# Gate and up projections as seven products of halves, with their weights held in DRAM

## The chip, the core and the metric

The kernel runs on one core of a Trainium2 chip. A core has five engines, each with an instruction queue of its own: TensorE (PE in the profile; PEld is its loading of stationary weights), VectorE (DVE), ScalarE (ACT), GpSimd (POOL) and SyncE (SP), which here only issues DMAs. The core's SBUF holds working data in 128 partitions, PSUM takes TensorE's results in eight banks of 512 float32 columns, and DRAM holds inputs, output and spilled tensors. Sixteen DMA engines move data between DRAM and SBUF. The metric is the device time of one execution in microseconds (us).

## The reference

A block over 8192 tokens of 448 channels: an AFNO spectral mixer and a GEGLU feed-forward network, both with adaptive layer norm.

```python
h = layernorm(x) * (1 + ca) + sa
x = x + ga * A(h)        # rfft over tokens, per-frequency 2-layer MLP, shrinkage, irfft
h = layernorm(x) * (1 + cb) + sb
x = x + gb * ((gelu(h @ w_gate) * (h @ w_up)) @ w_down)    # 448 -> 1792 -> 448
```

The sizes are N = 8192, D = 448, F = 1792. sa to gb are rows of silu(c) @ w_mod. Everything is float32 at the interface; the kernel splits float32 factors into a high and a low 16-bit part and takes three products (high by high, high by low, low by high).

## The kernel before

The program has three stages on one core: the forward transform over chunks of x, a spectral stage of 32 steps, and the FFN stage, which also ends the inverse transform.

**Spectral stage.** `step(i)` writes out, in a fixed order, the work of one step: `fetch_t` (loads `tr`), `stage_s2` (second transform: groups of three products of 128 columns, L368 to L370), the two MLP layers, `stage_i1`, and hooks ("load", "pe", "act", "dve", "pool") into which `at(step, hook, fn, ...)` puts side work. In steps 3 to 14 the side work loads gate and up weights, squares them and sums the squares with products against ones (`norms`, L711), for scales. From step 17 on, `load_w` loads one piece of 256 columns of w_gate or w_up per step, and `weights_hi` (ACT, L790) and `weights_lo` (DVE, L795) cast it into the resident tiles `wh` and `wl`, [128, 4, 3584] in fp16 each.

**FFN stage.** The work goes by blocks of 256 tokens (`CB` = 2 rows of 128; 32 blocks, index i). Within a block, t counts seven pairs of 128 hidden channels, tile t and tile t + 7 (q = 0, 1). `gate_up(i, k)` with k = 2t + q multiplies 128 hidden channels of gate and of up (pr = 0, 1) with 256 tokens. The 448 input channels are three full groups of 128 rows and one of 64; the high and low parts of the last 64 are packed so that ten products of 128 rows and 256 columns do for gate or for up, and what is left of the low weights of the last 64 rows is done for two values of t together, as a burst of eight products of 64 rows, in the upper or lower half of the array (all at L1087). Gate goes through a gelu on ACT (L1123), times up on DVE (L1128).

The down projection takes 2 x 2 halves (hidden tiles t and t + 7, output column halves, two token rows) and computes seven products instead of eight. Its left factors are the four quarters and four sums of them, made on POOL (L1134 to L1137); `quantize` casts them into high (ACT, L1145) and low (DVE, L1146) parts. `down(i - 1)` runs after k = 2 of block i: 7 x 7 x 3 products of 224 columns (L1153 to L1155), with copies and sums (L1176 to L1194) and `finish`, on POOL, which scales, adds the residual and hands the rows to the output DMA (L1197).

**Preparing a block.** Tables `hooks`, `second`, `ahead` and `first` place, by k, the steps that prepare the block two ahead: `load_v`, `load_g` (DMA), `split_v`, `split_g` (ACT, POOL), `inverse` (L987 to L989, TensorE), `residual`, `stats2`, `rsqrt_part`, `norm2` (L1036, L1037), `pack_hi`, `pack_lo`, and `transposes_dma` (L1057), in which SP issues four DMA transposes per block into `nts`. For block 0 the transposes are done by TensorE (L1069). Six of the seven down weight tiles are loaded and cast (`load_d8`, `down_hi` L920, `down_lo` L924) during the first block.

The order is written out by hand: each engine runs its instructions in the order of the program. All DMAs go through SP's queue, also in program order. PSUM has four tags, pa to pd, of two banks each, which `bank` hands out in turn; gate and up use pa and pb, down uses pd and pc.

## Time and profile before

| | us |
|---|---|
| median of 3 runs | 1941.13 (1939.67 to 1942.28) |
| the profiled execution: time | 1940.48 |
| its span in the profile | 1938.7 |
| TensorE busy in the span | 1903.1 |
| DVE / ACT / POOL busy | 1109.8 / 788.3 / 1159.4 |
| first and last start of a gate or up product | 385.0 and 1919.4 |

In the profile, a row of a group gives line, engine, operation, the tiles (out<-in), the shape, the count after "x", then busy time in us, the mean duration of one in ns, and the idle time of the engine before them with what ended it. Busy time counts overlapping instructions once, so count times mean can be more. A row of the timeline gives the start, the duration in us, engine, line and operation; neighbours of one line are merged, with their count. A row of a stretch of time gives its ends, its length, each engine's busy time with its instructions, the granted TensorE clock, the DMA engines' busy share and GB/s. A row of one line's instructions gives minimum, median and maximum duration in ns and the first and last start.

### The profile page before, as it was taken

To read this page: it belongs to the slowest core of one execution; us is meant where nothing else is said; L and a number is where in the kernel's file an instruction comes from. 1 tells how busy PE (TensorE), PEld (TensorE's weight loads), DVE (VectorE), ACT (ScalarE), POOL (GpSimd) and SP (SyncE) were. 2 spreads that over 40 slices of the span, in tenths; PEclk is the share of its full clock that TensorE was granted. 3 is DMA by queue.
4 is the path that set the end of the run, shared out by engine and by line. 5 is a ranking of instruction groups with operands and counts; after the bars stand their busy time and mean duration, and the time that the engine had idled before them with its cause. 6 is when DMAs were issued, how large, how long until landed. Compare 5 with 4: busy or idle time off the path is not lost.

```text
span 1938.7 us, 43005 instructions
## 1 busy us (share of the span) xinstructions
PE 1903.1 (98%) x17620; PEld 1694.9 (87%) x17620; DVE 1109.8 (57%) x2352; ACT 788.3 (41%) x1338; POOL 1159.4 (60%) x1466
## 2 busy tenths in 40 slices
PE   7899999899999999999999999999999999999999
PEld 3599999778888888888888888888888888888898
DVE  8677788786555555555555555555555555555533
ACT  5677888553333333333333333333333333333322
POOL 3157655256666666666666666666666666666644
PEclk9899999999999999999999999999999999999999
...
GB/s 346 314 286 257 203 188 197 171 140 49 45 43 45 43 41 45 45 41 46 41 46 43 42 44 44 43 43 44 43 44 43 43 43 43 43 43 43 21 11 20
DMA packets 157981, 163.79 MB, mean 84 GB/s; under 512 B 77908, under 2 KB 136152, under 8 KB 157784
## 3 DMA queue, kind: packets, MB, share of 16 engines
...
## 4 chain that ended last, share of the span: by engine, by line
PE 86%; DVE 4%; issue 3%; ACT 3%; DMA 2%; POOL 2%; SPq 1%; ACTq 0%; POOLq 0%; DVEq 0%
PE pgu L1087 53%; PE pdn L1155 8%; PE pdn L1154 8%; PE pdn L1153 8%; PE ps L202 2%; DVE y L463 2%; PE pi L989 1%; PE pi L988 1%; PE pi L987 1%; POOL yl L107 1%; DMA raw<-in_B_w_up 1%; DVE st L163 0%; ACT th L105 0%; PE ps L368 0%; PE ps L370 0%
## 5 line engine op out<-in xcount | busy, mean ns | idle before, releaser
L1087 PE MATMUL pgu<-nt,wh 128*128 128x256 f16 x6272 | 834.3, 273 | 2.7 <-DVE x L1128 2.6
L1087 PEld LDWEIGHTS <-wh 128*128 128x128 f16 x6272 | 602.7, 98 | 101.5 <-issue 33.9
L1123 ACT ACTIVATE gel<-pgu,dg 128x256 f32<-128x256 f32 x448 | 200.3, 473 | 792.3 <-PE pgu L1087 756.2
L1087 PE MATMUL pgu<-nt,wl 128*128 128x256 f16 (+1 forms) x3584 | 501.3, 272 | 0.4 <-DVE x L1128 0.4
L1155 PE MATMUL pdn<-wd,ac 128*128 128x224 f16 x1568 | 406.1, 259 | 0.2 <-DVE ac L1146 0.2
L1153 PE MATMUL pdn<-wd,ac 128*128 128x224 f16 x1568 | 406.1, 259 | 0.0
L1154 PE MATMUL pdn<-wd,ac 128*128 128x224 f16 x1568 | 406.1, 259 | 0.0
L1134 POOL TENSOR_TENSOR x<-x 128x128 f32<-128x128 f32 x223 | 239.9, 1076 | 260.3 <-DVE x L1128 228.1
L1146 DVE SCALAR_TENSOR_TENSOR ac<-x,sa_act,ac 128x896 f16<-128x896 f32 (+1 forms) x225 | 308.9, 1373 | 83.3 <-ACT ac L1145 83.3
L1087 PEld LDWEIGHTS <-wl 128*128 128x128 f16 (+1 forms) x3584 | 297.9, 97 | 57.5 <-issue 24.3
L1128 DVE TENSOR_TENSOR x<-pgu,gel 128x256 f32<-128x256 f32 x448 | 179.6, 418 | 276.2 <-ACT gel L1123 275.6
L1145 ACT ACTIVATE ac<-x,sa_act 128x896 f16<-128x896 f32 (+1 forms) x225 | 232.9, 1035 | 49.0 <-POOL x L1137 47.0
L1190 POOL TENSOR_TENSOR o<-u,p 128x224 f32<-128x224 f32 x32 | 21.0, 657 | 291.8 <-DVE u L1189 291.8
L1135 POOL TENSOR_TENSOR x<-x 128x128 f32<-128x128 f32 x223 | 157.5, 706 | 17.5
L1155 PEld LDWEIGHTS <-ac 128*128 128x128 f16 x1568 | 153.4, 98 | 0.5 <-DVE ac L1146 0.5
L1154 PEld LDWEIGHTS <-ac 128*128 128x128 f16 x1568 | 153.4, 98 | 0.4
L1153 PEld LDWEIGHTS <-ac 128*128 128x128 f16 x1568 | 153.4, 98 | 0.4
L107 POOL TENSOR_TENSOR yl<-y,yh 128x448 fp32r<-128x448 f32 x63 | 78.9, 1252 | 75.6 <-ACT yh L105 64.4
L463 DVE SCALAR_TENSOR_TENSOR y<-pm,t 64x224 f32<-64x224 f32 x256 | 99.5, 389 | 41.3 <-ACT t L455 37.4
L1136 POOL TENSOR_TENSOR x<-x 128x128 f32<-128x128 f32 x223 | 113.7, 510 | 0.0
L1137 POOL TENSOR_TENSOR x<-x 128x128 f32<-128x128 f32 x223 | 110.7, 497 | 0.0
L107 POOL TENSOR_TENSOR tl<-tr,th 128x896 f16<-128x896 f32 x30 | 57.3, 1909 | 68.3 <-DMA td<-xt 36.8
...
## 6 DMA issues: line engine op xcount, KB each, us to landing
...
```

The lines of the kernel that those rows point to most:

```text
L107: (el or V).tensor_tensor(lo, src, h, ALU.subtract)
L463: V.scalar_tensor_tensor(y[ri * 64 : ri * 64 + 64, gi], pv[si, ri], LAM, tv[si, ri], op0=ALU.add, op1=ALU.min)
L1087: T.matmul(pgu[i, t, q][:, pr * H : (pr + 1) * H], w[rows, tw, f0 : f0 + 128], nts[i][rows, tn, :], start=start, stop=stop, skip_group_che ...
L1123: S.activation(gl, ps[:, :H], AF.Gelu_apprx_tanh, scale=dg)
L1128: V.tensor_tensor(dst, ps[:, H : 2 * H].rearrange("p (b c) -> p b c", b=2), gl.rearrange("p (b c) -> p b c", b=2), ALU.mult)
L1134: e.tensor_tensor(s1, a21, a22, ALU.add)
L1135: e.tensor_tensor(s2, s1, a11, ALU.subtract)
L1145: S.activation(ac[:, 0, k], x[:, k], AF.Copy, scale=sc)
L1146: V.scalar_tensor_tensor(ac[:, 1, k], x[:, k], sc, ac[:, 0, k], op0=ALU.mult, op1=ALU.subtract)
L1153: T.matmul(ps, ac[:, 0, ka], wds[t][:, 0, kb], start=t == 0, stop=False)
L1154: T.matmul(ps, ac[:, 0, ka], wds[t][:, 1, kb], start=False, stop=False)
L1155: T.matmul(ps, ac[:, 1, ka], wds[t][:, 0, kb], start=False, stop=t == NP - 1)
```

## The change

Gate and up are no longer multiplied by 128-row products. For 384 of the 448 channels, the product of (two halves of the channels) x (hidden tiles t and t + 7) x (two token rows) is formed as seven products of halves instead of eight; the last 64 channels are multiplied directly. The channels are cut into pieces of 64 rows: gate's weights lie in partitions 0 to 63 and up's in 64 to 127, each with its copy of the tokens, and every step of 64 rows issues a product for gate in the upper half of the array and one for up in the lower half, of 128 columns each, into two banks.

- **Weights.** In the spectral stage `load_forms` loads the pieces of one t, `form_sums` makes the sums of quarters (POOL), `forms_hi` and `forms_lo` cast 23 pieces of 128 columns, and `store_forms` writes them to DRAM (`wsd`). In the FFN stage three slots hold the forms of three t. `torder` runs through t upward and downward in turn; `plan_slots` says which slot is refilled for which later unit, and `after` issues the load in two parts (12 and 11 pieces) when stage b or stage d of the unit that frees it has been issued.
- **Tokens.** `token_sums` makes sums of token pieces (DVE), and `transposes` issues twelve DMA transposes per block instead of four, for block 0 too.
- **Order of a unit.** A unit u is one t of one block. Its products come in four stages: a, b, c, d. `period(u)` interleaves stage a of u, stage d of u - 2, stage c of u - 1 and stage b of u. Between them ACT copies partial results (`copy_b`), seeds one region of PSUM with another (`seed`), DVE joins regions (`joins`), and gelu and product go over three quarters and one quarter (`gel3`, `mult3`, `gel1`, `mult1`). Three pairs of banks (`sets`) go round by u mod 3, the fourth (`pdn`) is for down.
- **Down.** All seven tiles are cast in the spectral stage. `down` uses pdn and the set `pf`, which the following unit's stage a takes; `phase(i)` runs the inverse transform, the residual, the loads of the block after, and down, after the third unit of a block.
- The scales of tokens and of gate and up weights are made for a smaller range (13 in place of 15 as the exponent), and a DMA scratch area in SBUF is cut to 2048 bytes.

```diff
+        def load_forms(t):
+            r = fp.tile([128, 14, 128], F32, tag="wr", name="wr", bufs=2)
+            for pr, rows in enumerate(rows2):
+                v = (wg, wu)[pr].rearrange("(k p) (q t f) -> p q k t f", p=64, q=2, t=NP)
+                for q in range(2):
+                    dma(r[rows, 6 * q : 6 * q + 6], v[:, q, 0:6, t])
+                dma(r[rows, 12:14], v[:, :, 6, t])
+            return r
+
+        def form_sums(t):
+            r = raws[("w", t)]
+            f = raws[("f", t)] = fp.tile([128, 9, 128], F32, tag="wf", name="wf")
+            a11, a12, a21, a22 = (r[:, 3 * j : 3 * j + 3] for j in range(4))
+            G.tensor_tensor(f[:, 3:6], a11, a21, ALU.subtract)
+            G.tensor_tensor(a21, a21, a22, ALU.add)
+            G.tensor_tensor(f[:, 0:3], a21, a11, ALU.subtract)
+            G.tensor_tensor(f[:, 6:9], a12, f[:, 0:3], ALU.subtract)
+
+        def form_cuts(t, part):
+            r = raws[("w", t)]
+            if part == 0:
+                return (slice(0, 9), r[:, 0:9]), (slice(18, 23), r[:, 9:14])
+            return ((slice(9, 18), raws[("f", t)]),)
+
+        def forms_hi(t, part):
+            for k, src in form_cuts(t, part):
+                S.activation(wslot[wat[t]][:, 0, k], src, AF.Copy, scale=sww)
+
+        def forms_lo(t, part):
+            for k, src in form_cuts(t, part):
+                w = wslot[wat[t]]
+                V.scalar_tensor_tensor(w[:, 1, k], src, sww, w[:, 0, k], op0=ALU.mult, op1=ALU.subtract)
+
+        def store_forms(t):
+            a = 0
+            for w, n in zip(wsd, WPARTS):
+                dma(w[t], wslot[wat[t]][:, :, a : a + n])
+                a += n
 
         wdp = wd.rearrange("(q t p) c -> t p q c", q=2, p=128)
...
         wpool = ctx.enter_context(tc.tile_pool(name="wpool", bufs=1))
-        wh = wpool.tile([128, 4, 2 * F], F16, name="wh")
-        wl = wpool.tile([128, 4, 2 * F], F16, name="wl")
+        wslot = [wpool.tile([128, 2, NWB, 128], F16, name=f"ws{s}") for s in range(2)]
...
         at(19, "dve", down_scales2)
-        for j in range(14):
-            at(17 + j, "load", pre, fp, ("w", j % 2, j // 2), load_w, j % 2, j // 2)
-            at(18 + j, "act", weights_hi, j % 2, j // 2)
-            at(18 + j, "dve", weights_lo, j % 2, j // 2)
-        at(30, "load", load_d4, fp, 0)
+        for n, t in enumerate(worder):
+            u = 18 + 2 * n
+            at(max(17, u - 2), "load", pre, None, ("w", t), lambda pool, t: load_forms(t), t)
+            at(u - 1, "pool", form_sums, t)
+            for part in range(2):
+                at(u + part, "act", forms_hi, t, part)
+                at(u + part, "dve", forms_lo, t, part)
+            if u + 2 < nu:
+                at(u + 2, "load", store_forms, t)
+        for t, u in enumerate([21, 23, 25, 27, 29, 30, 31]):
+            at(u - 1, "load" if u < 30 else "pool", load_d4, t)
...
+        torder = [t for i in range(nch) for t in (range(NP) if i % 2 == 0 else range(NP - 1, -1, -1))]
+        slot_of, refill = {}, {}
...
+        def plan_slots():
+
+            held = [[0 if wat[0] == s else 1, -1] for s in range(2)] + [[2, -1]]
+            for u, t in enumerate(torder):
+                s = next((n for n, (h, _) in enumerate(held) if h == t), None)
+                if s is None:
+                    s = min(range(3), key=lambda n: held[n][1])
+                    refill[held[s][1]] = u
+                    held[s][0] = t
+                slot_of[u] = wslot[s]
+                held[s][1] = u
+
+        plan_slots()
+
+        def load_part(u, part):
+
+            a, n = (0, WPARTS[0]), WPARTS
+            lo = a[part]
+            dma(slot_of[u][:, :, lo : lo + n[part]], wsd[part][torder[u]])
+
+        def after(u, part):
+
+            if u in refill:
+                load_part(refill[u], part)
 
...
-        def transposes_dma(i, gs=range(2)):
+        def token_sums(i, part):
+
+            n = nxt[i]["n"]
+            if part == 0:
+                nxt[i]["t"] = cp.tile([128, 13 * 64], F32, tag="tf", name="tf")
+            t = nxt[i]["t"]
+            b11, b21, x0 = n[:, 0, 0:192], n[:, 0, 192:384], n[:, 0, 384:448]
+            b12, b22, x1 = n[:, 1, 0:192], n[:, 1, 192:384], n[:, 1, 384:448]
+            t1, t2, t3, t4 = (t[:, 192 * j : 192 * j + 192] for j in range(4))
+            if part == 0:
+                V.tensor_tensor(t1, b12, b11, ALU.subtract)
+                V.tensor_tensor(t3, b22, b12, ALU.subtract)
+            else:
+                V.tensor_tensor(t2, b22, t1, ALU.subtract)
+                V.tensor_tensor(t4, b21, t2, ALU.subtract)
...
+        def transposes(i, gs):
+            if i not in nts:
+                nts[i] = cp.tile([128, 2, NXT, 128], F16, tag="nt", name="nt", bufs=2)
             for g in gs:
-                for b in range(CB):
-                    nc.sync.dma_start(
-                        nts[i][:, 4 * g : 4 * g + 4, b * 128 : (b + 1) * 128],
-                        nxt[i]["pk"][:, b, PKO[4 * g] : PKO[4 * g] + 512],
-                        transpose=True,
-                    )
-
...
+        def xblock(i, pr, n):
+            w, odd = divmod(n, 2)
+            if odd == pr:
+                return nts[i][rows2[pr], 0, w, :]
+            return nts[i][rows2[pr], 1, w if odd else (w - 1) % NXT, :]
+
+        def mm(u, ps2, reg, wb, x, xo, n, start=False):
+
+            i, slot = u // NP, slot_of[u]
+            for j in range(n):
+                for m, (hl, xb) in enumerate(((0, x[0]), (0, x[1]), (1, x[0]))):
+                    for pr, rows in enumerate(rows2):
+                        T.matmul(
+                            ps2[:, pr, reg * 128 : reg * 128 + 128],
+                            slot[rows, hl, wb + j, :],
+                            xblock(i, pr, xb + xo + j),
+                            start=start and j == 0 and m == 0,
+                            stop=j == n - 1 and m == 2,
+                            skip_group_check=True,
+                        )
+
+        RV, RY, RX = 0, 1, 2
+
+        def stage_a(u):
+            p = sets[u % 3]
+            mm(u, p, RY, 0, XB0, 0, 3, start=True)
+            mm(u, p, RV, 6, XT, 0, 3)
+            mm(u, p, RX, 3, XB0, 3, 3)
+
+        def stage_b(u):
+            mm(u, sets[u % 3], RY, 9, XT, 3, 3)
+
+        def stage_c(u):
+            p = sets[u % 3]
+            mm(u, p, RV, 12, XT, 6, 3)
+            mm(u, p, RV, 22, XB1, 6, 1)
+            mm(u, p, RY, 15, XB1, 3, 3)
+            mm(u, p, RY, 21, XB1, 6, 1)
+            mm(u, p, RX, 21, XB0, 6, 1)
+
+        def stage_d(u):
+            p = sets[u % 3]
+            mm(u, p, RV, 18, XT, 9, 3)
+            mm(u, p, RV, 22, XT, 12, 1)
+
+        sbs, cts = {}, {}
...
+        def copy_b(u):
+            sbs[u] = cp.tile([128, 2, 256], F32, tag="sb", name="sb", bufs=2)
+            S.copy(sbs[u], sets[u % 3][:, :, 0:256])
+
+        def seed(u):
+            p = sets[u % 3]
+            S.copy(p[:, :, 0:128], p[:, :, 128:256])
+
+        def joins(u):
+            p, b = sets[u % 3], sbs.pop(u)
+            c = cts[u] = cp.tile([128, 2, 3, 128], F32, tag="c", name="c")
+            V.tensor_tensor(
+                c[:, :, 1:3, :],
+                p[:, :, 0:256].rearrange("p g (r c) -> p g r c", r=2),
+                b[:, :, 0:128].rearrange("p g (o c) -> p g o c", o=1).to_broadcast([128, 2, 2, 128]),
+                ALU.add,
             )
-
...
+        def gel3(u):
+            gls[u] = cp.tile([128, 3, 128], F32, tag="gl3", name="gl3")
+            S.activation(gls[u], cts[u][:, 0], AF.Gelu_apprx_tanh, scale=dg)
+
+        def mult3(u):
+            xs[u] = cp.tile([128, 8, 128], F32, tag="x8", name="x8", bufs=4)
+            V.tensor_tensor(xs[u][:, 1::3, :], cts.pop(u)[:, 1], gls.pop(u), ALU.mult)
+
+        def gel1(u):
+            gls[u] = cp.tile([128, 128], F32, tag="gl1", name="gl1", bufs=2)
+            S.activation(gls[u], sets[u % 3][:, 0, 0:128], AF.Gelu_apprx_tanh, scale=dg)
+
+        def mult1(u):
+            V.tensor_tensor(xs[u][:, 0], sets[u % 3][:, 1, 0:128], gls.pop(u), ALU.mult)
+
+        def sums(u, e=G):
+            a12, a11, s1, s2, a22, s3, s4, a21 = (xs[u][:, j] for j in range(8))
+            e.tensor_tensor(s1, a21, a22, ALU.add)
...
-            b1, b2 = bank("pd", "pdn"), bank("pc", "pdn")
-
-            product(i, b1, 0, 0, range(NP - 1))
-            product(i, b2, 1, 1, range(NP - 1))
-            S.copy(p1, product(i, b1, 0, 0, [NP - 1]))
-            V.tensor_tensor(o11, product(i, b2, 1, 1, [NP - 1]), p1, ALU.add)
+            d0, d1, f0, f1 = (p[:, b, :] for p in (pdn, pf) for b in range(2))
+            heads = [(0, d0), (1, d1)] + ([(2, f0), (4, f1)] if last else [])
...
+            S.copy(p4, product(i, f0, 2, rest if last else range(NP)))
+            if not last:
+                mid(1)
+            V.tensor_tensor(u2, product(i, f1, 4, rest if last else range(NP)), p1, ALU.add)
+            V.tensor_tensor(u4, product(i, d0, 3), u2, ALU.add)
+            if not last:
+                mid(2)
+            p7 = product(i, d1, 5)
...
+            p3 = product(i, f0, 6)
             for b, h in ((1, 0), (1, 1), (0, 1)) if last else ((1, None), (0, None)):
                 if b == 0:
                     V.tensor_tensor(o12, p3, u4, ALU.add)
...
+        def period(u):
+            on(u, stage_a)
+            on(u - 1, seed)
+            on(u - 2, joins)
+            on(u - 2, gel3)
+            on(u - 4, quant_lo)
+            on(u - 2, mult3)
+            on(u, copy_b)
+            on(u - 2, stage_d)
+            on(u - 2, lambda v: after(v, 1))
+            on(u - 2, gel1)
+            on(u - 2, mult1)
+            on(u - 2, lambda v: sums(v, V if v == NT_ - 1 else G))
+            on(u - 3, quant_hi)
+            on(u - 1, stage_c)
+            on(u, stage_b)
+            on(u, lambda v: after(v, 0))
+
...
+        def phase(i):
+
+            u = i * NP + LA
+            pf = sets[(u + 1) % 3]
+            j = i + 2
+            on(u - 3, quant_lo)
+            if j < nch:
+                inverse(j, pf)
+                residual(j)
+                loads(j + 1)
...
+            if i > 0:
+                down(i - 1, pf, mid)
+
+        extra = {
+            0: [(2, split_v)],
+            1: [(2, split_g), (1, transposes, range(0, 4))],
+            2: [(1, transposes, range(4, 12))],
+            3: [(2, token_sums, 0), (2, pack_hi, [0]), (2, pack_lo, [0])],
+            4: [(2, token_sums, 1), (2, pack_hi, [1]), (2, pack_lo, [1])],
+            5: [(2, pack_hi, [2]), (2, pack_lo, [2])],
+            6: [(2, pack_hi, [3]), (2, pack_lo, [3])],
```

401 lines of the change are left out of this document (179 added, 222 removed).

## The prediction

> **What bounds the kernel now.** I read the page first (busy shares, then the chain), then long stretches, then single products in the timeline.
>
> ```profile
> span 1938.7 us, 43005 instructions
> PE 1903.1 (98%) x17620; PEld 1694.9 (87%) x17620; DVE 1109.8 (57%) x2352; ACT 788.3 (41%) x1338; POOL 1159.4 (60%) x1466
> PE pgu L1087 53%; PE pdn L1155 8%; PE pdn L1154 8%; PE pdn L1153 8%; PE ps L202 2%; DVE y L463 2%; PE pi L989 1%; PE pi L988 1%; PE pi L987 1%; POOL yl L107 1%; DMA raw<-in_B_w_up 1%; DVE st L163 0%; ACT th L105 0%; PE ps L368 0%; PE ps L370 0%
> ```
> ```profile
> 480.00:1890.00 1410.00, 1409.84 (x13488) 1263.11 (x13486) 725.21 (x1433) 455.62 (x756) 900.41 (x1162) 1.00 0.15 42
> ```
> The second fence is one stretch of the FFN: busy time of PE, weight loads, DVE, ACT, POOL, then the granted clock (1.00), the DMA share (0.15) and GB/s. TensorE is never free; the others are half idle or more. Gate and up are 53% of the chain, the down product 24%. A busy PE need not be at its peak, so its pace comes from starts in the timeline: ten full products, 256 columns each, then a stretch with a shared burst of half-height products (8 of the 11), the down product from its first start to the next gate product, and the inverse transform; below them, from SP's timeline, two starts of the transposes, three blocks apart.
>
> ```profile
> 1000.56 0.93 PE L1087 MATMUL pgu<-nt,wh 128*128 128x256 f16 x7
> 1001.32 0.49 PE L1087 MATMUL pgu<-nt,wl 128*128 128x256 f16 x3
> 1001.65 0.27 PE L1087 MATMUL pgu<-nt,wh 128*128 128x256 f16 x1
> ...
> 1004.60 1.03 PE L1087 MATMUL pgu<-nt,wl 128*128 128x256 f16 x11
> 1005.56 0.50 PE L1087 MATMUL pgu<-nt,wh 128*128 128x256 f16 x3
> ...
> 1012.12 0.26 PE L1153 MATMUL pdn<-wd,ac 128*128 128x224 f16 x1
> ...
> 1026.21 0.49 PE L1087 MATMUL pgu<-nt,wh 128*128 128x256 f16 x3
> ...
> 1035.52 0.45 PE L987 MATMUL pi<-vh,gh 128*128 128x448 f32 x1
> ...
> 1036.84 0.94 PE L1087 MATMUL pgu<-nt,wh 128*128 128x256 f16 x7
> ```
> ```profile
> 867.02 6.40 SPq L1057 DMA_TRANSPOSE nt<-pk  x4
> ...
> 1011.37 5.13 SPq L1057 DMA_TRANSPOSE nt<-pk  x4
> ```
> Ten products take 1001.65 − 1000.56 = 1.09 us, 109 ns each. A block has 7 x 40 of them: 30.5 us. A burst costs 1005.56 − 1004.60 less three full products, 0.63 us; 3.5 per block: 2.2 us. Down takes 14.1 us, the inverse transform 1.3. Sum 48.1; the transposes say (1011.37 − 867.02)/3 = 48.1. Nothing but products is in a block.
>
> **The change: TensorE.** A unit (a block's pair of 128-channel tiles t and t+7) now has 25 steps of 64 rows in stages a (9), b (3), c (9), d (4), each in three high/low products for gate and for up: 75 pairs of 64-row, 128-column products, 16,800 pairs in all. What a pair costs decides the case. The trace has pairs at 256 columns (the half bursts), 128-column products at full height (L368 to L370), and dense loads (the norms):
>
> ```profile
> L1087 PE MATMUL pgu<-nt,wl 64*128 64x256 f16 x896 | 68.6, 272 | 0.4 <-DVE x L1128 0.4
> L711 PEld LDWEIGHTS <-sq 128*128 128x128 bf16 x84 | 4.1, 97 | 1.1 <-issue 0.2
> 345.83 0.22 PE L369 MATMUL ps<-s,th 128*112 128x128 f16 x1
> ...
> 346.90 0.22 PE L370 MATMUL ps<-s,tl 128*112 128x128 f16 x1
> ```
> The 896 half products are 112 bursts of 8 and fill 68.6 us, 0.61 us a burst; one after another 8 would need 7 x 0.109 + 0.27 = 1.03, as four pairs 3 x 0.109 + 0.27 = 0.60. So halves do run two at a time. From 345.83 to 346.90 are 19 intervals: 56 ns for 128 columns, a new weight load each. I take 56 ns per pair: 525 pairs per block = 29.6 us against 30.5 + 2.2. The unseen part is that four instructions must start per 56 ns, where these rows sustain two. L711 gives the nearest dense case: 28 groups of three loads fill 4.1 us, (4.1/28 − 0.097)/2 = 25 ns from load to load with a product between, two in 50 ns; that is why I take 56. The ends are 50 ns and 112 ns, the latter (+941 us) if starts keep today's two per 56.
>
> Each burst's two changes between full and half height cost (0.63 − 4 x 0.109)/2 = 0.1 us; instead of 3.5 round trips a block there is one around the inverse and down: +0.1 beside the row above, the return lying under the next wait. Down's last product now goes to a bank of the set that the next stage a fills, so TensorE waits for L1194 to empty it: the rest of that product (0.26 us) + 0.39 + a handover, 0.65 us. Before, other banks stood ready. Between 0 (the wait hidden) and 1.0 (one more 0.39 us operation of DVE ahead).
>
> **The other engines.** Per unit, from these rows (mean ns of one):
>
> ```profile
> L1145 ACT ACTIVATE ac<-x,sa_act 128x896 f16<-128x896 f32 x204 | 211.8, 1038 | 41.3 <-POOL x L1137 41.0
> L1123 ACT ACTIVATE gel<-pgu,dg 128x256 f32<-128x256 f32 x408 | 182.5, 473 | 739.5 <-PE pgu L1087 705.2 <-DVE rcy L118 23.9 <-DVE x L1128 10.4
> L1176 ACT COPY p<-pdn 128x224 f32<-128x224 f32 x30 | 10.4, 346 | 109.8 <-PE pdn L1155 109.8
> L1146 DVE SCALAR_TENSOR_TENSOR ac<-x,sa_act,ac 128x896 f16<-128x896 f32 x204 | 283.8, 1391 | 73.5 <-ACT ac L1145 73.5
> L1128 DVE TENSOR_TENSOR x<-pgu,gel 128x256 f32<-128x256 f32 x408 | 163.5, 418 | 254.8 <-ACT gel L1123 254.1
> L1194 DVE TENSOR_TENSOR o<-pdn,u 128x224 f32<-128x224 f32 x29 | 11.4, 391 | 38.4 <-PE pdn L1155 38.4
> L1134 POOL TENSOR_TENSOR x<-x 128x128 f32<-128x128 f32 x204 | 225.3, 1105 | 206.0 <-DVE x L1128 206.0
> L1135 POOL TENSOR_TENSOR x<-x 128x128 f32<-128x128 f32 x204 | 141.5, 694 | 16.0
> L1136 POOL TENSOR_TENSOR x<-x 128x128 f32<-128x128 f32 x205 | 103.8, 506 | 0.0
> L1137 POOL TENSOR_TENSOR x<-x 128x128 f32<-128x128 f32 x205 | 98.4, 480 | 0.0
> ```
> ACT had two gelus and one quantization (2.0 us); now seed 0.38, gelu over 384 columns 0.58, copy over 512 0.60, gelu over 128 0.37, quantization 1.04: 3.0. DVE had 2.2; now joins 0.68 + 0.42, products 0.55 + 0.29, quantization 1.39: 3.3 (sizes that no row has are estimates, by columns from the rows). POOL's four sums stay, 2.8. A period of TensorE is 75 x 56 ns = 4.2 us, so all three fit, DVE with 0.9 to spare. The order fits too: if stage a starts at 0, copy_b is done at 2.2 and stage b needs it at 3.7; joins, done near 1.0, free stage d at 1.5; seed, done at 0.6, serves stage c at 2.2; mult1 at 3.1 frees the set for 4.2. A block's extra work (split, pack, token sums, norms, residual) goes mostly beside the 14 us of down. I put in 0.25 us per block, between 0 and 0.9 (DVE's spare run out once).
>
> **Weights from DRAM.** Slots hold three of seven tiles and every second block runs backwards, so four tiles of 1.5 MB are fetched per block, each in two parts.
>
> ```profile
> 0.00:100.00 100.00, 81.57 (x325) 49.09 (x326) 73.34 (x264) 56.70 (x120) 24.54 (x42) 0.93 0.95 331
> L1057 SPq DMA_TRANSPOSE nt<-pk x124: 1198/1251/2534, 409.1 to 1837.1; - x124
> 1030.65 0.35 SPq L1197 DMA_DIRECT2D out<-x  x1
> ```
> At the 331 GB/s of the first 100 us a part needs 2.3 us, the block 18 of 46. Transposes go from 4 to 12 per block, 15 us of SP's queue; they are issued ahead of down and needed a block later. The tight place is after down: out waits for POOL until 1030.65 − 1026.21 = 4.4 us past down's end, and parts queue behind it on SP. The second part for three units on is ready at 2.8, goes at about 5, lands near 9 to 10 and is needed near 11 (0.65 + 2 x 4.2 + 2.2). It holds, by 1 to 2 us, so I price it at nothing.
>
> A block is then 29.6 + 14.1 + 1.3 + 0.1 + 0.65 + 0.25 = 46.0 us, 2.1 less, x 32 = 67 us.
>
> **Once only.** In the spectral stage each tile's forms are summed on POOL, cast, stored and all seven down tiles are cast there.
>
> ```profile
> 260.00:340.00 80.00, 79.25 (x742) 76.44 (x742) 66.60 (x126) 66.72 (x114) 44.50 (x30) 1.00 0.74 196
> L790 ACT ACTIVATE wh<-raw,sw x14: 1149/1175/1179, 237.6 to 348.0; 128x1024 f16<-128x1024 f32 x14
> L795 DVE SCALAR_TENSOR_TENSOR wl<-raw,sw,wh x14: 1272/1309/1314, 242.8 to 368.2; 128x1024 f16<-128x1024 f32 x14
> L920 ACT ACTIVATE wd<-dr,dsc x12: 840/942/1042, 386.6 to 424.1; 128x672 f16<-128x672 f32 x6, 128x896 f16<-128x896 f32 x6
> L924 DVE SCALAR_TENSOR_TENSOR wd<-dr,dsc,wd x12: 910/1127/1345, 387.4 to 429.0; 128x672 f16<-128x672 f32 x6, 128x896 f16<-128x896 f32 x6
> L1087 PE MATMUL pgu<-nt,wh x6272: 269/273/421, 385.0 to 1919.1; 128*128 128x256 f16 x196
> 379.40 0.69 DVE L1037 SCALAR_TENSOR_TENSOR n<-n,r,sb_r 128x448 f32<-128x448 f32 x1
> ```
> A step is (348.0 − 237.6)/13 = 8.5 us, with 7.1 of DVE and of ACT. Per step DVE loses 1.3 and gains 1.9 (1472 columns for 1024, half of five instructions) + 1.1: 8.8, over the step; ACT comes to 7.1 − 1.2 + 1.6 + 0.9 = 8.4. DMA gets 15 MB more in 119 us: 0.74 + 126/331 x 0.95 = 1.10 of what it can do, +12 us. I take 12; 4 to 25. Then the norm is done at 380.1; before, products begin at 385.0. Now token sums and packing end near 383.5 and twelve transposes of 1.25 us run on SP where TensorE did them: ten are needed, so about 396, +11 (to +16), and a cold clock +2. The first block streams weights without a down product to hide them, about 8, but the 8 us that today go to casting down weights there are gone. The tail, +2. Sum +27.
>
> The profiled execution took 1940.48 us (span + 1.8; the median, 1941.13, is 0.65 above): 1940.5 − 67 + 27 = 1900.
>
> **Rivals.**
> - *Starts (the other side).* TensorE's sequencer can't start four instructions per 56 ns. For: nothing sustained is denser than two. Against: L711's 25 ns. It decides at 40 us/16,800 = 2.4 ns, a pair at 58.4. At 62 ns it is +101 us: 2001.
> - *Weights come late.* Parts queue behind out and behind each other; a late part stops stage a or c. For: 1 to 2 us to spare, DMA share from 0.15 to about 0.7. Against: 331 GB/s seen. It turns the sign at 40/32 = 1.25 us per block; at 2 us: 1964.
> - *Covers fail.* DVE or ACT queues run 0.9 us per block late: 1929.
> - *Loads set the pace.* If a pair can't begin before its loads have ended, it takes their 97 ns (the mean in L711's row), 41 more: 1900 + 689 = 2589. Against: the 56 ns from product to product in L368 to L370, each with its own load. The Trainium skill, TensorE: Matmul & The Clock Gate, Back-to-back issue gap, has a rule of this kind: in a stream of loads and products both set the spacing, some 81 ns at 128 columns. By that figure the sum would be 1900 + 25 x 16.8 = 2320; the trace disagrees at full height, and no run here shows half height at 128 columns.
>
> **How the numbers follow.** Forecast 0.54 (its own range 1870 to 1928), covers 0.08 (0.06 faster, 0.01 same, 0.01 slower), late weights 0.16 (0.03 same), starts 0.18, loads 0.04. Faster 0.60, within 0.2% (3.9 us, what a measurement can tell) 0.04, slower 0.36. The range 1868 to 2000 takes in forecast, covers, late weights and half of starts.
>
> **What would show it.** Right: pairs 56 ns apart from pair to pair in the timeline, a block of 46 us between the transposes of following blocks, about 0.7 us before the first stage a after down, DMA share near 0.7, the first gate product near 405 to 410. Wrong: pairs at 59 ns or more; TensorE idle ahead of stages a or c, released by a DMA on a slot; idle ahead of b or d, released by ACT or DVE.

## The result, and the profile after

The changed kernel takes 2526.76 us (median of 4 runs, 2517.62 to 2532.90) against 1941.10 us of the kernel before: ratio 1.3014, 95% interval 1.2972 to 1.3056. I had forecast 1900, in a range up to 2000. The profiled execution has a span of 2526.9 us. The page of the changed kernel, busy shares, granted clock in 40 slices, and the lines of the chain:

```profile
span 2526.9 us, 92738 instructions
PE 2034.0 (80%) x41348; PEld 1893.0 (75%) x41348; DVE 1459.9 (58%) x2958; ACT 1047.3 (41%) x1917; POOL 1107.1 (44%) x1531
PEclk9757657777777999999999999999999999999999
PE pb L1164 11%; PE pa L1164 11%; PE pc L1164 11%; PE pd L1264 4%; PE pd L1266 3%; PE pd L1265 3%; DVE y L470 2%; SPq L1148 1%; DVE x L1226 1%; ACT t L462 1%; PE pc L448 1%; PE pb L421 1%; PE pa L375 1%; ACT th L112 1%; DVE c L1210 1%
```

TensorE was 98% busy and is 80% busy; products have left the chain for gaps, and the granted clock is at 5 to 7 tenths in slices 2 to 13 (63 us each). The same stretches as before (busy time of PE, weight loads, DVE, ACT, POOL, granted clock, DMA share, GB/s), one of the spectral stage and one of the FFN:

```profile
260.00:340.00 80.00, 55.02 (x353) 50.83 (x352) 27.38 (x62) 29.56 (x48) 26.14 (x25) 0.65 0.43 119
...
1000.00:1800.00 800.00, 713.25 (x18264) 685.37 (x18260) 540.32 (x1044) 351.33 (x670) 435.26 (x624) 0.98 0.71 176
```

In the first, 353 products where there were 742, with every other engine less busy too and DMA's share at 0.43 where it was 0.74: no engine is the limit there, so they wait for one another. Where the stages begin and how long a block is, from the views of single lines (count, shortest, median and longest ns, first and last start in us): the weight loads of gate and up after, the stores of the output after, the same stores before.

```profile
L1164 PEld LDWEIGHTS <-ws x33600: 92/94/148, 801.2 to 2508.9; 64*128 64x128 f16 x199
```
```profile
L1315 SPq DMA_DIRECT2D out<-x x31: 338/344/366, 898.3 to 2483.5; - x31
```
```profile
L1197 SPq DMA_DIRECT2D out<-x x31: 332/348/353, 451.6 to 1898.0; - x31
```

The first gate product comes at 801.2 instead of 385.0: +416. A block takes (2483.5 − 898.3)/30 = 52.8 us instead of (1898.0 − 451.6)/30 = 48.2: +4.6, times 32 is +148. The first block and the tail make up the other 24 of the span's 588. So there are two losses, and neither is in the products: in the timeline a run of 54 (27 pairs) starts 1.51 us before the next one, 55.9 ns a pair.

```profile
1500.33 1.67 PE L1164 MATMUL pc<-nt,ws 64*128 64x128 f16 x54
1501.84 0.83 PE L1164 MATMUL pa<-nt,ws 64*128 64x128 f16 x24
```

What TensorE waits for in the spectral stage (100 to 795 us: total, times, longest), and in the FFN (1000 to 1800):

```profile
PE pc L448 <- DVE y L470: 112.6, 32, 6.1
PE pb L421 <- DVE hl L439: 51.6, 27, 4.1
PE pa L375 <- DVE zl L384: 42.4, 27, 1.6
```
```profile
PE pa L1164 <- issue: 18.0, 15, 2.7
PE pb L1164 <- issue: 17.8, 14, 2.5
PE pc L1164 <- issue: 16.0, 13, 2.7
PE pd L1264 <- DVE u L1302: 7.2, 15, 0.5
PE pd L1264 <- ACT p L1292: 6.5, 15, 0.4
```

Each row of the spectral stage is the first product of a new result waiting for the *reader* of the result before it. The hunk of the change that can make this so is the one on PSUM: a tag had two tiles of one bank and has one tile of two; the experiments test it. In the FFN the down product waits in the same way, for readers of the bank beside its own; and 52 us go to "issue", where nothing that the profile shows is waited for. Both kinds in the timeline, first the four places in one down product and behind it, then two "issue" stops inside a stage:

```profile
1515.27 0.26 PE L1264 MATMUL pd<-wd,ac 128*128 128x224 f16 x1 [0.43 <-ACT p L1292]
...
1518.17 0.26 PE L1264 MATMUL pb<-wd,ac 128*128 128x224 f16 x1 [0.43 <-ACT p L1298]
...
1522.83 0.26 PE L1264 MATMUL pd<-wd,ac 128*128 128x224 f16 x1 [0.48 <-DVE u L1302]
...
1527.50 1.68 PE L1164 MATMUL pb<-nt,ws 64*128 64x128 f16 x54 [0.48 <-DVE o L1312]
...
1538.95 0.55 PE L1164 MATMUL pc<-nt,ws 64*128 64x128 f16 x13
1540.47 1.34 PE L1164 MATMUL pc<-nt,ws 64*128 64x128 f16 x41 [0.96 <-issue]
...
1556.28 0.27 PE L1164 MATMUL pb<-nt,ws 64*128 64x128 f16 x3
1558.19 1.62 PE L1164 MATMUL pb<-nt,ws 64*128 64x128 f16 x51 [1.64 <-issue]
```

The stop at 1540.47 ends 2.38 us, the one at 1558.19 ends 2.32 us after a packet of the DMA queue "instruction" begins. That queue's packets in the trace:

```
start us   bytes   took ns
1538.09    16384   967
1542.67    16384   974
1546.68    16384   959
1550.59    16384   945
1555.87    16384   912
```

```profile
q8 instruction: 323, 5.29, 0.9%
```

The page's row counts 323 such packets; 2 x 41,348 instructions of TensorE make 256 each. So TensorE's program comes in pieces of 256 instructions. Before, such a piece lasted 13.4 us (median between two packets); at four instructions per 56 ns it lasts 3.6. Below, a gap of over 0.25 us between starts of products that ends 2.2 to 3.05 us after such a packet's start is called a late fetch; they are summed from the trace's records over 15 blocks behind 1000 us. After has 4.3 us of them per block, before 0.06. The block without any of its gaps is 44.6 us.

Two counts in the trace say that these stops are at the pieces' borders and have to do with the weights. When TensorE's loads, products and semaphore instructions are numbered in order, 89 of the 101 late fetches behind 1000 us have one and the same number modulo 256. And at these borders inside dense stretches (the piece before it under 5.5 us long, 1000 to 1800 us), 40 of 62 came late, 62.0 us in all, where over 20 packets of weight parts (3072 or 2816 bytes) start between 1.5 us before and 1.0 us after the start of the fetch's packet; where there are fewer, 8 of 53, 3.6 us.

### The profile page after: what moved, and what is told of

Its sections match the earlier page's. It is cut to its first block, busy times and chain, and to the rows that moved or that the text cites. A ratio compares the mean times of both kernels' runs of the same rounds, so it can differ in the third digit from the quotient of the medians.

```text
span 2526.9 us, 92738 instructions
## 1 busy us (share of the span) xinstructions
PE 2034.0 (80%) x41348; PEld 1893.0 (75%) x41348; DVE 1459.9 (58%) x2958; ACT 1047.3 (41%) x1917; POOL 1107.1 (44%) x1531
## 4 chain that ended last, share of the span: by engine, by line
PE 67%; DVE 13%; issue 7%; ACT 7%; DMA 3%; SPq 2%; POOL 1%; ACTq 0%; DVEq 0%; POOLq 0%
PE pb L1164 11%; PE pa L1164 11%; PE pc L1164 11%; PE pd L1264 4%; PE pd L1266 3%; PE pd L1265 3%; DVE y L470 2%; SPq L1148 1%; DVE x L1226 1%; ACT t L462 1%; PE pc L448 1%; PE pb L421 1%; PE pa L375 1%; ACT th L112 1%; DVE c L1210 1%
## 5 line engine op out<-in xcount | busy, mean ns | idle before, releaser
L1164 PEld LDWEIGHTS <-ws 64*128 64x128 f16 x33600 | 965.7, 95 | 197.6 <-issue 186.2
L1164 PE MATMUL pa<-nt,ws 64*128 64x128 f16 x11250 | 384.4, 219 | 64.0 <-issue 37.0
L1164 PE MATMUL pb<-nt,ws 64*128 64x128 f16 x11250 | 386.7, 219 | 51.5 <-issue 40.7
L1164 PE MATMUL pc<-nt,ws 64*128 64x128 f16 x11100 | 379.9, 218 | 50.4 <-issue 38.3
L1254 DVE SCALAR_TENSOR_TENSOR ac<-x,sa_act,ac 128x896 f16<-128x896 f32 x224 | 317.8, 1419 | 19.8 <-ACT ac L1245 19.8
L1222 ACT ACTIVATE gl<-c,dg 128x384 f32<-128x384 f32 x224 | 138.0, 616 | 400.8 <-DVE c L1216 385.8
L1264 PE MATMUL pd<-wd,ac 128*128 128x224 f16 x896 | 233.3, 260 | 30.2 <-DVE u L1302 15.4
L1266 PE MATMUL pd<-wd,ac 128*128 128x224 f16 x896 | 232.7, 260 | 1.8 <-DVE ac L1254 1.0
L1265 PE MATMUL pd<-wd,ac 128*128 128x224 f16 x896 | 232.7, 260 | 0.8 <-issue 0.8
L1245 ACT ACTIVATE ac<-x,sa_act 128x896 f16<-128x896 f32 x224 | 231.2, 1032 | 0.6 <-DVE x L1240 0.4
L1237 POOL TENSOR_TENSOR x<-x 128x128 f32<-128x128 f32 x223 | 105.6, 474 | 271.6 <-DVE x L1226 271.6
L1226 DVE TENSOR_TENSOR x<-c,gl 128x384 f32<-128x384 f32 x224 | 181.6, 811 | 31.0 <-ACT gl L1222 31.0
L1240 POOL TENSOR_TENSOR x<-x 128x128 f32<-128x128 f32 x223 | 129.2, 579 | 19.2 <-DVE x L1233 18.9
```

The lines of the kernel that those rows point to most:

```text
L1164: T.matmul(ps2[:, pr, reg * 128 : reg * 128 + 128], slot[rows, hl, wb + j, :], xblock(i, pr, xb + xo + j), start=start and j == 0 and m == ...
L1222: S.activation(gls[u], cts[u][:, 0], AF.Gelu_apprx_tanh, scale=dg)
L1226: V.tensor_tensor(xs[u][:, 1::3, :], cts.pop(u)[:, 1], gls.pop(u), ALU.mult)
L1237: e.tensor_tensor(s1, a21, a22, ALU.add)
L1240: e.tensor_tensor(s4, a12, s2, ALU.subtract)
L1245: S.activation(acts[u][:, 0], xs[u][:, 0:7], AF.Copy, scale=sa_act[:, t : t + 1])
```

## The experiments

Theory A: the two-bank tile takes away the double buffering, since a product into one bank is made to wait for the readers of the other, in the spectral stage and in down. Rival B: the spectral stage is longer by the work and the traffic put into it. Theory F: the "issue" stops are instruction fetches that come late beside the weight parts. Rival G: a fetch is too slow for 14 ns an instruction in any case. Each time below is that of one run, beside the kernel before at 1938 to 1940 us, unless an interval stands there.

**The PSUM hunk alone, in the kernel before** (before_pairs).

```diff
-    psum = ctx.enter_context(tc.tile_pool(name="psum", bufs=2, space=bass.MemoryType.PSUM))
+    psum = ctx.enter_context(tc.tile_pool(name="psum", bufs=1, space=bass.MemoryType.PSUM))
+    banks2 = {tag: psum.tile([128, 2, 512], F32, name=tag) for tag in ("pa", "pb", "pc", "pd")}
+    turn = dict.fromkeys(banks2, 0)
     def bank(tag, name):
-        return psum.tile([128, 512], F32, tag=tag, name=name)
+        turn[tag] += 1
+        return banks2[tag][:, turn[tag] % 2, :]
```

> The kernel before with one hunk of the change alone: each PSUM tag is one tile of two banks, of which slices are handed out in turn, in place of two tiles of one bank. Theory A (a product into one bank of such a tile waits for the readers of the other): the spectral stage loses what it lost in the changed kernel, so the first gate product moves from 385 to 700 to 800 us and the total is 2250 to 2450 us, with the waits of PE on DVE zl, hl and y that the changed kernel shows. Rival B (the spectral stage is long because of the forms, the casts, the stores and the DMA traffic that were added to it): nothing moves, 1941 us within 10.

2742 us. First gate product at 771.8, and the three waits of the changed kernel are there under this kernel's line numbers:

```profile
PE pc L444 <- DVE y L466: 94.8, 32, 3.6
PE pa L371 <- DVE zl L380: 44.0, 28, 1.6
PE pb L417 <- DVE hl L435: 38.6, 27, 1.6
```

B is out as the main cause. The total is above what I expected because this kernel's FFN takes all its banks from the hunk too: 61.3 us a block. A hunk that adds no work costs 800 us.

**The hunk undone in the spectral stage of the changed kernel** (split_banks): two one-bank tiles per tag in a pool that closes at the end of the stage, then the two-bank tiles.

```diff
-    psum = ctx.enter_context(tc.tile_pool(name="psum", bufs=1, space=bass.MemoryType.PSUM))
-    banks2 = {tag: psum.tile([128, 2, 512], F32, name=tag) for tag in ("pa", "pb", "pc", "pd")}
+    pctx = ExitStack()
+    psum = pctx.enter_context(tc.tile_pool(name="psum", bufs=2, space=bass.MemoryType.PSUM))
...
     mctx.close()
+    pctx.close()
     with ExitStack() as cctx:
+        psum = cctx.enter_context(tc.tile_pool(name="psum2", bufs=1, space=bass.MemoryType.PSUM))
+        banks2 = {tag: psum.tile([128, 2, 512], F32, name=tag) for tag in ("pa", "pb", "pc", "pd")}
```

> The changed kernel, but with two tiles of one bank per PSUM tag up to the end of the spectral stage, as before; the FFN keeps its two-bank tiles. Theory A: the first gate product comes at 395 to 430 instead of 801 us, and the total falls by 370 to 405 us to 2120 to 2160; the FFN itself keeps its 1726 us. Rival B: the first gate product stays after 650 us and the total above 2370.

2166 us, and the first gate product at 449.1: −352 of the 416. The granted clock of 100 to 200 us goes from 0.62 back to 1.00 (979 products instead of 391). The rest of the delay, 64 us, is more than A allowed for and is taken up below.

```profile
L1165 PEld LDWEIGHTS <-ws x33600: 91/94/149, 449.1 to 2146.5; 64*128 64x128 f16 x199
```

**No fetching of weights** (split_banks_no_reload). The kernel leaves out the refills of the slots, so most units multiply by the weights of another tile and the output is not the block's; the products are as many as before.

```diff
         def after(u, part):
-            if u in refill:
-                load_part(refill[u], part)
+            pass
```

> The run with separate banks in the spectral stage, and the weight tiles are not fetched again from DRAM in the FFN (the slots keep what they hold after the first three tiles, so most units multiply by the weights of another tile). Theory F (TensorE's instruction fetches, 16 KB for 256 instructions, come late because they share the DMA engines with the weight parts): the idle stretches inside the stages that the profile puts down to nothing but issue, about 3.8 us a block, go, and the FFN is 100 to 125 us shorter, about 1610. Rival G (a fetch takes too long for 14 ns an instruction with or without other traffic): the idle stretches stay and the FFN is within 25 us of 1726.

2020 us; the FFN is 1578 us of span instead of 1715, the block 48.4 instead of 52.4. In 1000 to 1800 no "issue" row is left among the larger waits of products (50.4 us in split_banks), late fetches go from 4.3 to 0.5 us a block (5 of the 22 gaps that are left behind 1000 us stand at a border, of 73 in split_banks 62), and the DMA share is 0.30. F holds, G does not: fetches keep up with 14 ns an instruction when the DMA engines are quieter. A block gains 4.0 us, a little more than the 3.8 that I had counted, and the whole 138 us instead of 100 to 125.

**Down's banks as tiles of their own** (down_banks). This and all later kernels keep the separate banks of the spectral stage.

```diff
-        pdn = banks2["pd"]
+        pdn = [psum.tile([128, 512], F32, name=f"pd{n}") for n in range(2)]
...
-            d0, d1, f0, f1 = (p[:, b, :] for p in (pdn, pf) for b in range(2))
+            d0, d1, f0, f1 = *pdn, pf[:, 0, :], pf[:, 1, :]
+            g4, g3, g5, g6 = (f1, d0, d1, f0) if last else (d0, d1, d0, d1)
...
-            V.tensor_tensor(u4, product(i, d0, 3), u2, ALU.add)
+            V.tensor_tensor(u4, product(i, g3, 3), u2, ALU.add)
```

Products 4, 5 and 6 take g4, g5 and g6 in the same way. So the edit does two things, tiles of one bank and another order of banks, and the runs do not part them.

> The run with separate banks in the spectral stage, and in the FFN the two banks of the down product are tiles of their own; the products 2, 4, 3, 5, 6 go to the set's first bank, then in turn to down's two banks, so that none follows a reader of its own bank by less than one product, and the last one is not in the bank that the next stage a fills. Theory A says 3 waits of 0.6 and one of 0.74 us per block go: 2.5 us a block, the FFN 70 to 80 us shorter, some 1650, total 2045 to 2085. If the waits only move to the next thing that is late, the FFN is less than 30 us shorter.

2084 us, the block 50.1: −2.3. The waits in down and the one on L1312 behind it are gone; what is left is "issue" and the joins (c):

```profile
PE pb L1165 <- issue: 17.9, 14, 3.0
PE pc L1165 <- issue: 13.1, 11, 2.6
PE pa L1165 <- issue: 10.7, 9, 2.4
PE pb L1165 <- DVE c L1217: 4.3, 9, 0.7
```

**Weights in other pieces.** quarter_parts, on down_banks; four_slots_halves, on four_slots (below), is the same with 64 for 32:

```diff
-            dma(slot_of[u][:, :, lo : lo + n[part]], wsd[part][torder[u]])
+            for p in range(0, 128, 32):
+                rows = slice(p, p + 32)
+                dma(slot_of[u][rows, :, lo : lo + n[part]], wsd[part][torder[u], rows])
```

> The run down_banks (2084 us, its FFN 1636 from the first gate product at 446.9), with each weight part fetched as four DMAs of 32 partitions in place of one of 128: the same bytes in the same packets. Theory H (an instruction fetch stands in line behind the packets of one part on its DMA engine, 16 of 0.12 us): a quarter has 4 packets there, and between two quarters on SP's queue lies an issue of some 0.6 us, so a fetch is late by less; of the idle stretches that end 2.2 to 2.6 us after a fetch's packet, 50 us in 1000 to 1800, at least half go, and the total falls by 40 to 90 us. Rival I (only the bytes and the share of the DMA engines count): those stretches stay at 40 to 60 us and the total within 20 of 2084.

> The run four_slots (2040 us, late fetches 40 us in 1000 to 1800) with each weight part as two DMAs of 64 partitions. Theory H (fetches wait behind the packets of one part): with 8 packets instead of 16 per engine the late stretches halve to some 20 us in 1000 to 1800, total 1995 to 2025. Rival M (more DMAs on SP's queue make the weights themselves late, as the quarters did): waits of PE on ws appear, total 2040 or more.

2312 and 2144 us: both worse, and theory H falls. The late fetches do not halve (4.0 and 4.2 us a block; 3.2 and 2.7 in down_banks and four_slots): the stretches just end a little later behind the packet, 2.7 us, so that the narrow window of my expectation missed them. SP issued the pieces directly one behind another, so they may have stood in one line together; that is argued, not shown. Rival I had the stretches right and the total wrong. With quarters the weights come late as well (rows of quarter_parts, 1000 to 1800):

```profile
PE pb L1167 <- DMA ws<-wsd: 24.4, 12, 4.5
PE pc L1167 <- DMA ws<-wsd: 23.3, 12, 4.1
```

**A fourth slot** (four_slots), on down_banks, so that three tiles are fetched per block and not four.

```diff
-        wslot.append(cp.tile([128, 2, NWB, 128], F16, name="ws2"))
+        for s in (2, 3):
+            wslot.append(cp.tile([128, 2, NWB, 128], F16, name=f"ws{s}"))
...
-            gls[u] = cp.tile([128, 128], F32, tag="gl1", name="gl1", bufs=2)
+            gls[u] = cp.tile([128, 128], F32, tag="gl1", name="gl1")
```

> The run down_banks with a fourth weight slot in SBUF (the room comes from the second buffer of gl1): three tiles of seven are fetched per block instead of four, a quarter fewer bytes. Theory F (instruction fetches late behind weight parts): the late fetches fall in proportion, the block by 0.6 to 1.2 us, total 2045 to 2068. If the weight parts' own lateness or the sequencer is what counts, under 10 us.

2040 us, the block 48.5; late fetches 2.7 us a block instead of 3.2, "issue" of the products 26.6 us instead of 41.7. The gain is 1.6 us a block, more than F's 0.6 to 1.2: late fetches account for 0.5 of it and other gaps for 0.7; the granted clock of 1000 to 1800 us also rises from 0.98 to 1.00.

**Spacing the traffic.** four_pieces_spaced, on four_slots, asks for each part behind its own stage, and puts the output's store behind the next unit's parts:

```diff
-WPARTS = (12, 11)
+WPARTS = (6, 6, 6, 5)
...
             on(u, stage_a)
+            on(u, lambda v: after(v, 0))
...
-            on(u - 2, lambda v: after(v, 1))
+            on(u - 2, lambda v: after(v, 3))
...
             on(u - 1, stage_c)
+            on(u - 1, lambda v: after(v, 2))
             on(u, stage_b)
-            on(u, lambda v: after(v, 0))
+            on(u, lambda v: after(v, 1))
+            for args in outs:
+                dma(*args)
+            outs.clear()
```

transposes_in_threes adds the first of these edits to it; transposes_under_down has the second one on four_slots:

```diff
-            1: [(2, split_g), (1, transposes, range(0, 4))],
-            2: [(1, transposes, range(4, 12))],
+            0: [(2, split_v), (1, transposes, range(0, 4))],
+            1: [(2, split_g), (1, transposes, range(4, 8))],
+            2: [(1, transposes, range(8, 12))],
...
-                sw_, c = divmod(g, NXT // 4)
+                c, sw_ = divmod(g, 2)
```
```diff
-            1: [(2, split_g), (1, transposes, range(0, 4))],
-            2: [(1, transposes, range(4, 12))],
+            1: [(2, split_g)],
+            2: [(1, transposes, range(0, 12))],
```

> The run four_slots with each tile's weights in four parts of 6, 6, 6 and 5 of its 23 column blocks, each asked for as soon as its own stage (a, b, c, d) has read the old ones, so the parts are spaced by TensorE's own progress; and the store of a block's output stands on SP's queue behind the next unit's parts, not ahead of them. The bytes are the same, the DMAs twice as many. Theory H2 (a fetch waits for the whole line of packets that stands on the DMA engines when it is asked for, and a part of 12 blocks is 1.9 us of line): the line is never over 0.9 us, less than the 1.2 us that a fetch can be late, and the late fetches, 2.9 us a block in four_slots, fall below 1.2; total 1965 to 2000. Theory N (the number of DMAs, or the bytes, counts): they stay at 2.9 or more, total 2035 or more.

> The run four_pieces_spaced with the twelve transposes of a block in three groups of four (5 us of SP's queue each), behind the units 0, 1 and 2 of the block, in place of four and eight. Theory H2 (the line of packets): parts leave nearer to their release, the line is shorter, late fetches fall from 2.4 to 1.5 us a block or less, total 1995 to 2015. Theory N (the bytes): 2.2 to 2.6 us, total 2030 to 2040.

> The run four_slots with all twelve transposes of a block issued just ahead of the down product (15 us of SP's queue beside its 14 us of TensorE, where 256 instructions last some 12 us) and none beside the units. If any packets beside the dense units make fetches late, whatever they carry (theory N in its wide form), the late fetches fall from 2.7 to 2.0 to 2.4 us a block, total 2015 to 2030. If only the weight parts do: 2.5 to 2.9 us and 2035 to 2045.

2036, 2044 and 2067 us, late fetches 2.4, 3.5 and 3.0 us a block. H2 finds no support. Transposes beside dense units make fetches late too: in transposes_in_threes 14 of the 56 us lost at borders in 1000 to 1800 us stand where hardly a weight packet runs. Moving them all under down does not help either, perhaps because the parts that become ready meanwhile leave in a bunch behind 15 us of transposes; that is argued, not shown. Fewer bytes help. Cutting and ordering the same bytes otherwise gained at most 0.3 us a block of late fetches over four_slots, no more than sums_behind_joins (below, 2.4), which leaves the weights as they are. That is within what single runs can tell: sums_early (below), whose FFN stage is written as that of four_slots, has a block of 49.2 us against 48.5.

**The rest of the spectral stage.** Four edits: casts_after_split (on down_banks) has DVE's casts behind hl in a step; sums_early (on four_slots) has that, and the loads and POOL's sums a step earlier; no_reload_no_store (on down_banks) leaves out the fetches and six of seven stores, so its output is not the block's either; down_casts_late (on down_banks) takes down's loads and casts out of the stage.

```diff
-            hook("dve")
+            if i < 17:
+                hook("dve")
             if 0 <= i - 1 < nu:
                 stage_m1(*units[i - 1])
+            if i >= 17:
+                hook("dve")
```
```diff
-            at(max(17, u - 2), "load", pre, None, ("w", t), lambda pool, t: load_forms(t), t)
-            at(u - 1, "pool", form_sums, t)
+            at(max(17, u - 3), "load", pre, None, ("w", t), lambda pool, t: load_forms(t), t)
+            at(max(17, u - 2), "pool", form_sums, t)
...
-            f = raws[("f", t)] = fp.tile([128, 9, 128], F32, tag="wf", name="wf")
+            f = raws[("f", t)] = fp.tile([128, 9, 128], F32, tag="wf", name="wf", bufs=2)
...
-    nc = _bacc.Bacc("TRN2", target_bir_lowering=False, num_devices=1, dynamic_dma_scratch_size=2048)
+    nc = _bacc.Bacc("TRN2", target_bir_lowering=False, num_devices=1, dynamic_dma_scratch_size=1024)
```
```diff
-            for w, n in zip(wsd, WPARTS):
+            for w, n in zip(wsd, WPARTS) if t == 2 else []:
                 dma(w[t], wslot[wat[t]][:, :, a : a + n])
```
```diff
-        for t, u in enumerate([21, 23, 25, 27, 29, 30, 31]):
-            at(u - 1, "load" if u < 30 else "pool", load_d4, t)
-            at(u, "act", down_hi, t)
-            at(u, "dve", down_lo, t)
...
         drain()
+        for t in range(NP):
+            load_d4(t)
+            down_hi(t)
+            down_lo(t)
```

> The run down_banks, with the DVE casts of the weight forms and of down's weights in the spectral stage put behind stage m1's own DVE work (hl) of the step in place of ahead of it. Theory J (the spectral stage is 57 us longer than before because a cast of 2.2 to 3.5 us stands on DVE's queue ahead of hl, for which TensorE waits some 4 us every second step): the first gate product comes at 395 to 425 in place of 447 us, total 2040 to 2065. Rival K (the sum of DVE's work, or the DMA traffic, sets the step's length): still at 440 or later, total 2075 to 2095.

> The run four_slots with, in the spectral stage, the loads of a weight tile's forms and POOL's sums one step of the pipeline earlier (a second buffer for the sums), and DVE's casts behind hl as in casts_after_split. Theory L (the casts of ACT stand on its queue waiting for POOL's sums, 23 us in casts_after_split, and hold up hh, hl and so TensorE): the first gate product comes at 405 to 435 in place of 452 us, total 1995 to 2025. Rival K (the sum of work or the DMA traffic): 445 or later.

> Down's banks as in down_banks, no weight tile is fetched again in the FFN (as in split_banks_no_reload), and of the seven tiles only the one that the third slot starts with is stored to DRAM in the spectral stage. Rival K in its DMA form (the stores and other traffic set the pace there): the last product of the spectral stage, at 434 in split_banks_no_reload, comes 15 us earlier or more. If it is the order of the work on POOL, ACT and DVE: within 5 us of 434. For the FFN: with neither late fetches nor down's bank waits a block takes 44 to 45 us, 1 to 2 less than the 46.0 that I had predicted, the FFN 1490 to 1510 and the total 1935 to 1955; anything near 46.9 a block would say that another cost stays.

> The run down_banks with the loads and casts of down's seven weight tiles behind the spectral stage's last step, one tile after another, instead of in seven of its steps. If these casts (2.0 us of DVE and 1.8 of ACT in half of the steps) are what makes the spectral stage 57 us longer, its last product comes at 400 to 415 in place of 440 us; if the forms alone do it, at 425 to 440. The total is no aim here: the casts now stand open, 30 to 60 us.

The marker is the last start of the inverse product of the stage, one line in every kernel; here before, down_banks, down_casts_late, four_slots and sums_early:

```profile
L495 PE MATMUL pi<-yh,mil x66: 273/363/373, 105.0 to 368.6; 128*128 128x448 f32 x62, 128*128 128x224 f32 x4
```
```profile
L500 PE MATMUL pi<-yh,mil x66: 272/363/575, 106.0 to 424.1; 128*128 128x448 f32 x62, 128*128 128x224 f32 x4
```
```profile
L500 PE MATMUL pi<-yh,mil x66: 274/366/575, 103.6 to 401.1; 128*128 128x448 f32 x62, 128*128 128x224 f32 x4
```
```profile
L500 PE MATMUL pi<-yh,mil x66: 273/363/575, 106.7 to 425.9; 128*128 128x448 f32 x62, 128*128 128x224 f32 x4
```
```profile
L500 PE MATMUL pi<-yh,mil x66: 273/365/575, 105.4 to 412.9; 128*128 128x448 f32 x62, 128*128 128x224 f32 x4
```

So 55 us of delay here: 23 go with down's loads and casts, 13 with the earlier sums; casts behind hl alone gain nothing (427.1, total 2093). Single markers are good to some 5 us: eight kernels with the same spectral stage have it at 417.9 to 427.7, the four with the earlier sums at 411.9 to 414.7. The stores show no cost: 421.0 without and 417.9 with them. What TensorE and ACT wait for (down_banks, 250 to 440 us, then down_casts_late, 250 to 400):

```profile
PE pm L448 <- DVE hl L437: 25.0, 10, 4.1
ACT wd L957 <- DMA dr<-in_B_w_down: 4.9, 2, 2.8
ACT wd L957 <- DMA dr<-sd: 2.6, 2, 2.3
```
```profile
PE pm L448 <- DVE hl L437: 9.1, 4, 2.3
```

So most of it is the work put on POOL, ACT and DVE and its order there; ACT's 7.5 us for down's weights are DMA, and the run does not part these loads from the casts. The gaps take the clock with them (0.86 in 300 to 440 us of split_banks). About 20 us, with the casts of the forms themselves, were not taken apart. The expected 400 to 415 and 405 to 435 were missed: 401.1 is the marker alone (the last product, behind the open casts, came at 451.8, total 2117), and sums_early began the gates at 439.2, total 2046.

no_reload_no_store took 1962 us, the block 46.6, not the 44 to 45 expected: 2.2 us of gaps stayed, 1.5 of them ahead of stage d in two units.

**DVE behind down.** sums_behind_joins (on four_slots) puts the token sums behind the unit's joins and products; all_together adds four_pieces_spaced and sums_early; all_spread is all_together with transposes_in_threes, and gives each of the last four units its own share (`cut`) of the five subtractions.

```diff
             on(u - 2, mult1)
+            for fn, *args in mid:
+                fn(*args)
...
-            period(u)
             i, k = divmod(u, NP)
+            period(u, [(token_sums, i + 2, k - 3)] if k in (3, 4) and 0 < i < nch - 2 else [])
```
```diff
+            cut = {3: (0, 1), 4: (1, 2), 5: (2, 3), 6: (3, 5)}
+            period(u, [(token_sums, i + 2, k - 3, cut[k])] if k in cut and 0 < i < nch - 2 else [])
```

> The run four_slots with the token sums of the next block (1.7 and 1.6 us of DVE, in two units) behind that unit's joins and products on DVE's queue, not at the end of the unit before, ahead of its joins. If the waits of 0.6 and 0.9 us ahead of stage d in two units of each block are these sums on DVE's queue, both go: 1.2 to 1.6 us a block, total 1990 to 2005. If DVE has too little room in these units wherever the sums stand, less than 0.5 us a block, total 2025 or more.

> The two runs beside it and sums_early in one kernel: the first gate product at 430 to 445 us, a block of 45.3 to 46.5 us, total 1900 to 1945 if H2 holds, 1970 to 2000 if it does not.

> The same, with the earlier sums and later casts of sums_early in the spectral stage, and the token sums spread over the last four units of a block, one or two of DVE's five subtractions in each behind the unit's own joins and products. First gate product at 430 to 442 us. If DVE has room for 0.5 us in each unit, the waits of 0.6 and 0.9 us in two units of each block fall to under 0.5 together: with H2 a block of 46.0 to 47.0 us and a total of 1925 to 1960; with N 1970 to 2000.

2032, 2025 and 2039 us; the blocks of the last two, 48.7 and 49.0, and their totals lie outside all that I expected. Moving the sums within their units changes nothing (gaps that are not late fetches 1.25 us a block, 1.11 in four_slots); with them spread these are 0.39. all_spread moves the transposes too, which alone lowers TensorE's waits for the joins in 1000 to 1800 us (6.3 us in transposes_in_threes, 12.0 in four_pieces_spaced); but repaired_change (below) has no such wait at all, where transposes_under_down, with its transposes in the same place, has 15.7. So it was the amount of DVE work in two units. The gain is eaten by late fetches, 3.5 us with the transposes beside the units.

**Everything mended** (repaired_change): all_spread with the transposes placed by this edit.

```diff
-            0: [(2, split_v), (1, transposes, range(0, 4))],
-            1: [(2, split_g), (1, transposes, range(4, 8))],
-            2: [(1, transposes, range(8, 12))],
+            0: [(2, split_v)],
+            1: [(2, split_g)],
+            2: [(1, transposes, range(0, 12))],
...
-                c, sw_ = divmod(g, 2)
+                sw_, c = divmod(g, NXT // 4)
```

> Four slots, four spaced parts, the transposes all ahead of down, the earlier sums in the spectral stage, the token sums spread over four units, down's banks and the spectral stage's banks as tiles of their own. First gate product at 430 to 442 us, late fetches 1.8 to 2.4 us a block, waits for joins under 0.5: a block of 46.8 to 47.6 us, total 1955 to 1990, 1 to 2.5% slower than the kernel before; below 1940 only if the late fetches fall under 1 us a block.

2041.02 us (6 runs, 2035.21 to 2048.00), ratio to the kernel before 1.0504, 95% interval 1.0485 to 1.0522. In the profiled execution, the slowest of the six, late fetches are 3.7 us a block, other gaps 0.5, and the last product of the spectral stage comes 45 us later than before. Neither the 1955 to 1990 nor the fetches came out as expected. No version beat the kernel before; the lowest that computes the block was all_together with 2025 us.

## Why the prediction was wrong

- *The PSUM hunk* is the step that failed most. The account part by part has no term for it; the only sentence on banks, "Before, other banks stood ready", was applied to the wait behind down alone. It cost 352 us in the spectral stage, and in down 2.3 us a block with the wait that I did price (down_banks, which also changed the order of the banks). That wait was right: 0.74 us from start to start at 1527.50, against 0.65 + 0.1.
- *Weights "It holds, by 1 to 2 us, so I price it at nothing"*. Their arrival did hold, and the DMA share was 0.71 as forecast. What I did not ask is whom this traffic delays: TensorE's own instruction fetches, 4.3 us a block in the changed kernel; without the traffic the FFN is 138 us shorter. The rival "weights come late" named the right stream and the wrong victim.
- *Products at 56 ns*: right, 55.9. The rivals "starts" and "loads set the pace" are out as they were put; the sequencer starts four instructions per 56 ns, but not when its next 256 are missing. The Trainium skill, TensorE: Matmul & The Clock Gate, Back-to-back issue gap, would have had 81 ns; this trace, with 55.9, disagrees.
- *The block's work*, 29.6 + 14.1 + 1.3 = 45.0 us: right, 44.6 without gaps in the changed kernel.
- *The covers*, 0.25 with a bound of 0.9: mis-sized. The joins' waits are 0.6 and 0.9 us in two units where nothing else is late, 1.5 a block. I spread DVE's extra work over down; the token sums lie behind it.
- *Spectral stage +12 (4 to 25), by DMA*: mis-sized and the wrong cause. With banks apart the marker is 55 us later; the stores show no cost, and some 36, if the two gains add, go with down's loads and casts and the earlier sums, for the most part a matter of work and order on POOL, ACT and DVE. I compared sums of busy time with a step's length, 8.8 with 8.5, where a chain of three in-order queues was what mattered.
- *Start +11*: somewhat too much. From the end of block 0's norm to the first gate product are 4.9 us before (380.1 to 385.0) and 11.5 in split_banks (437.54 to 449.09), +7; in four_slots 15.3, +10. The +2 for the clock was not measured by itself.

Put together for the block: 44.6 + 4.3 late fetches + 2.3 to 2.5 bank waits + about 1.5 joins and small gaps = 52.7 to 52.9, of 52.8. Still open: why a fetch is late (spacing, order and size of the pieces did not tell), and some 20 us of the spectral stage.
